# Equal units of 288 tokens in the first stage of an attention and two-layer MoE kernel, and phi with its token chunks innermost

## The chip, the cores and the metric

The kernel runs on one core of a Trainium2 chip. The metric is the device time of one execution in microseconds (us), the median of the runs shown. TensorE is called PE, its weight loads PEld, VectorE DVE, ScalarE ACT, GpSimd POOL; SP is the engine that issues all DMAs, and its queue is SPq.

## What is computed

```python
# q, k, v (8, 8, 576, 64); phi (8, 8, 576, 32)
a = exp(phi - max over s); a = a / sum over m
k_m = einsum('bhsm,bhsd->bhmd', a, k);  v_m likewise with v
attn = softmax(q @ k_m.T / 8) ; x = attn @ v_m      # 4608 tokens x 512
r = max(x @ w_in, 0); x = (s * r * r + b) @ w_out   # 512 -> 2048 -> 512
h = x @ w1; x = (h * sigmoid(1.702 h)) @ w2         # 512 -> 2048 -> 512
```

## The kernel before

Four stages follow one another on the core, each overlapping a little with the next. **Stage 1** goes over the 8 batches of 576 tokens. For each batch `slots` (L420) takes the softmax weights of phi and the 32 slots of every head, `attend` and `weigh` (L487, L514) make the attention weights of all 576 tokens as two tiles `ah` and `al` (the value split into a high and a low half in fp32r), `matrix` (L561) multiplies v_m by a fourth of w_in into `mh` and `ml`, and `step` (L581) multiplies the two and applies relu. A step is one pair of 128-column groups of the 2048 hidden columns (8 pairs, `pi`) and one unit of tokens: 12 matmuls by `mm3` (L276), which takes three products (high by high, high by low, low by high) for two groups and two halves of the contraction. The result `h` in PSUM is copied with relu to an SBUF tile `r` (L598) and written to DRAM. **Stage 2** (`down` with w_out, L622) reads r back in 12 blocks of 384 tokens, two at a time, squares them on ACT (L642) and multiplies by w_out with seven products instead of eight on 2x2 blocks; the operands A, B, C, D and E are such blocks of r. **Stage 3** (`up`, L731) and **stage 4** (`down` with w2) work on the same blocks of 384.

The order of work is made by `Order` (L31): every piece has a due time and a cost in each engine that may do it, and a list scheduler places them, holding back what finds no free buffer. It writes one fixed order for each engine, and each engine keeps to it. In this planner a matmul costs n / 2.4 + 13.4 ns for n columns (L246). Tiles come from pools by tag: 31 of tag "t" (r, the operands, kv, q and others), 30 of "w", 4 of "ps" in PSUM (L180).

The blocks of 384 tokens of stage 2 do not meet the 576 tokens of a batch, so `units` (L216) cuts each batch where a block ends: even batches into 384 and 192 tokens, odd ones into 192 and 384. A unit of 384 is a whole block in DRAM, one of 192 half of one:

```python
n = min(self.TS - t % self.TS, self.S * (b + 1) - t)
to = ("r", s, pi % 4, pi // 4, half)
self.dram(*to).rearrange("p (a t) -> p a t", a=2)[:, :, at:at + n]
```

`load` (L618) brings a whole block of 384 KB back with one DMA. In `slots` phi comes as [128 tokens, 4 heads, 5 chunks of tokens, 32 slots]; `fmx` (L429) takes the maximum over the 5 chunks through a view that steps 32 numbers, `sub` (L433) subtracts the maximum, and `mm` (L449) takes the 32 slots of a chunk and head, contiguous, as the stationary operand for 40 matmuls with k and v. Batch 0's scores are made in two groups, the first unit first; all later batches make both units at once.

Of the kernel before, what the change touches and what calls it, by code (L numbers as in the profile page):

```python
# [152 lines left out]
class Net:  # L153
# [35 lines left out]
    def __init__(self, nc, tc, ctx, aps):  # L189
        self.nc, self.tc, self.a = nc, tc, aps  # L190
        self.B, self.S = aps["q"].shape[0], aps["q"].shape[3]
        self.sb = ctx.enter_context(tc.tile_pool(name="sb", bufs=1))
        self.ps = ctx.enter_context(tc.tile_pool(name="ps", bufs=1, space=PSUM))
        self.dr = ctx.enter_context(tc.tile_pool(name="dr", bufs=1, space=bass.MemoryType.DRAM))
        self.n = self.spare = 0
        self.T = {}
        self.order = Order(self.BUFS)
        self.d = {}
# [16 lines left out]

    def units(self, b):  # L216

        t = self.S * b
        while t < self.S * (b + 1):
            n = min(self.TS - t % self.TS, self.S * (b + 1) - t)  # L220
            m = t // self.TS
            yield t - self.S * b, n, m // 2, m % 2, t % self.TS
            t += n
# [196 lines left out]
    def slots(self, b, g, due, lead=8):  # L420
# [5 lines left out]
        pm, pb, z, tr = (("ps", ("s", b, g, i)) for i in range(4))  # L426
        self.dma(d - lead, lambda: self.t(ph, [P, 4, 5, 32]), lambda: self.a["phi"][b, g], (), (ph,), 320)

        def fmx():  # L429
            nc.vector.tensor_reduce(self.t(mx, [P, P]).rearrange("p (h m) -> p h m", h=4),  # L430
                                    T[ph].rearrange("p h c m -> p h m c"), axis=AX.X, op=ALU.max)

        def sub():  # L433
            pbv = T[pb][:, 0, 0:P].rearrange("p (h m) -> p h m", h=4).unsqueeze(2).to_broadcast([P, 4, 5, 32])
# [14 lines left out]
        def mm():  # L449
            out = self.pst(z)  # L450
            n = self.S - 4 * P
            for c in range(5):
                for h in range(4):
                    s = slice(32 * h, 32 * h + 32)
                    if c < 4:
                        nc.tensor.matmul(out[s, 0, 0:129], T[ph][:, h, c, :], T[fs[h]][:, c], start=(c == 0), stop=False)
                    else:
                        nc.tensor.matmul(out[s, 0, 0:129], T[ph][0:n, h, c, :], T[f1][0:n, h], start=False, stop=True)

# [120 lines left out]

    def step(self, b, pi, u, unit, due):  # L581
        nc, T = self.nc, self.T
        h, r = ("ps", ("h", b, pi, u)), ("t", ("r", b, pi, u))
        j = pi // 2
        c0, n, s, half, at = unit
        c = slice(c0, c0 + n)
        m = [("w", (x, b, j)) for x in ("mh", "ml")]
        ats = [[("t", (x, b, k)) for x in ("ah", "al")] for k in range(2)]

        def mm():  # L590
            out = self.pst(h)
            for i in range(2):
                o = slice((2 * pi + i) % 4 * P, (2 * pi + i) % 4 * P + P)
                self.mm3(out[:, i, 0:n], [([T[x][:, k, o] for x in m], [T[x][:, c] for x in ats[k]]) for k in range(2)])

        self.pe(due, n, mm, (*m, *((*x, u) for k in ats for x in k)), (h,), count=12)
        self.order.add(due + 0.5, [
            self.act(2 * n, lambda: nc.scalar.activation(self.two(r, n=n), T[h][:, :, 0:n], AF.Relu), psum=True),  # L598
            self.dve(2 * n, lambda: nc.vector.tensor_scalar(self.two(r, n=n), T[h][:, :, 0:n], 0.0, None, op0=ALU.max))], (h,), (r,))
# [17 lines left out]

    def load(self, due, k, name, *index):  # L618
        r = [x for x in self.order.wrote if x[:1 + len(index)] == (name, *index)]
        self.dma(due, lambda: self.two(k).rearrange("p a b -> p (a b)"), lambda: self.dram(name, *index), r, (k,), 384)  # L620

# [109 lines left out]
    def up(self, s, due):  # L731
# [4 lines left out]
        for j, k in ((0, 0), (1, 0), (0, 1), (1, 1)):  # L736
            self.load(due - 26 + 2 * j + 4 * k, R[j, k], "x", s, j, k)
        r11, r12, r21, r22 = R[0, 0], R[0, 1], R[1, 0], R[1, 1]
# [86 lines left out]
    def plan(self):  # L825
# [8 lines left out]
        for b in range(B):  # L834
# [5 lines left out]
            for j in range(4):  # L840
# [119 lines left out]
```

## Time and profile before

| | us |
|---|---|
| median of 3 runs | 1403.19 |
| lowest, highest | 1402.94, 1405.13 |
| the profiled execution | 1407.16 |
| its span in the trace | 1405.2 |
| PE busy | 1381.0 (98%) |
| DVE busy | 1041.4 (74%) |
| ACT busy | 795.8 (57%) |
| DMA queue of SP, share of 16 engines | 71.0% |

PE is busy nearly all of the span, but its time is the sum of matmuls of several shapes, and a busy PE need not be at its peak: the ends of matmuls are modelled and neighbours overlap, so that what one costs is the distance from its start to the start of the next. Stage 1 lasts until about 350 us on PE, with matmuls of stage 2 mixed in from about 330 us.

### The profile page before, as it was taken

The numbers are of one execution on the slowest core, as the hardware profiler recorded it, in microseconds if no ns is written. First come the engines' busy times: TensorE is split into PE (matmuls) and PEld (weight loads), VectorE is DVE, ScalarE is ACT, GpSimd is POOL, SyncE is SP. The second block draws the span as 40 slices with busy tenths as digits, with TensorE's granted clock in tenths as the row PEclk, the third lists the DMA queues.
The fourth block names the chain that finished last, engine by engine and source line by source line (L and its number), as shares of the span: only waits on it lengthen the run. The fifth ranks groups of instructions, "written<-read, shape, count | busy, mean of one in ns | idle before, by whom it ended". The sixth has DMA issues, their size and how long they took to land.

```text
span 1405.2 us, 23985 instructions
## 1 busy us (share of the span) xinstructions
PE 1381.0 (98%) x9250; PEld 1328.2 (95%) x9250; DVE 1041.4 (74%) x1411; ACT 795.8 (57%) x1113; POOL 92.0 (7%) x70
## 2 busy tenths in 40 slices
PE   7899999999999999999999999999999999999998
PEld 6788888789999999999999999999999999999998
DVE  6959898786698888988876756565356967869682
ACT  4456665576677787687745655554335434434341
POOL 1401110100100100000110110100000000000000
PEclk9999999999999999999999999999999999999999
DMA  9979999899875585499979674764896465344541
GB/s 349 305 255 302 378 368 332 291 311 358 280 246 187 182 277 173 153 320 320 337 261 345 259 271 166 257 238 147 277 360 242 155 195 177 125 158 162 195 138 45
DMA packets 134576, 347.74 MB, mean 247 GB/s; under 512 B 14400, under 2 KB 30784, under 8 KB 134464
## 3 DMA queue, kind: packets, MB, share of 16 engines
q1 hardware_dynamic: 134464, 346.24, 71.0%
q8 instruction: 72, 1.18, 0.3%
q14 instruction: 40, 0.33, 0.1%
HBM read 211.44 MB, written 134.74 MB: 246 GB/s over the span
## 4 chain that ended last, share of the span: by engine, by line
PE 85%; DMA 7%; DVE 6%; ACT 1%; issue 1%; SPq 1%; ACTq 0%; DVEq 0%
PE X L667 9%; PE X L669 9%; PE X L668 9%; PE Y L668 4%; PE Y L669 4%; PE Y L667 4%; PE X L774 4%; PE X L775 4%; PE X L776 4%; PE h L280 4%; PE h L282 4%; PE h L281 4%; PE Z L669 2%; PE Z L667 2%; PE Z L668 2%; DMA w<-w 2%
## 5 line engine op out<-in xcount | busy, mean ns | idle before, releaser
L282 PE MATMUL h<-ah,ml 128*128 128x384 f32 (+1 forms) x512 | 157.1, 307 | 5.5 <-DVE ml L264 5.5
L280 PE MATMUL h<-ah,mh 128*128 128x384 f32 (+1 forms) x512 | 161.0, 314 | 0.8 <-ACT km L258 0.5
L264 DVE TENSOR_TENSOR u<-Y,u 128x768 f32<-128x768 f32 x60 | 57.4, 956 | 135.5 <-ACT u L782 69.5
L281 PE MATMUL h<-al,mh 128*128 128x384 f32 (+1 forms) x512 | 156.6, 306 | 0.7 <-DVE al L264 0.7
L667 PE MATMUL X<-oh,wo 128*128 128x384 f32 x384 | 129.2, 337 | 2.9 <-ACT u L693 2.9
L774 PE MATMUL X<-oh,w 128*128 128x384 f32 x384 | 128.5, 335 | 1.1 <-ACT a L782 0.7
L668 PE MATMUL X<-ol,wo 128*128 128x384 f32 x384 | 129.0, 336 | 0.0
L669 PE MATMUL X<-oh,wo 128*128 128x384 f32 x384 | 128.8, 336 | 0.0
L776 PE MATMUL X<-oh,w 128*128 128x384 f32 x384 | 128.3, 334 | 0.0
L775 PE MATMUL X<-ol,w 128*128 128x384 f32 x384 | 128.3, 334 | 0.0
L667 PE MATMUL X<-oh,w 128*128 128x384 f32 x384 | 128.3, 334 | 0.0
L668 PE MATMUL X<-ol,w 128*128 128x384 f32 x384 | 128.3, 334 | 0.0
L669 PE MATMUL X<-oh,w 128*128 128x384 f32 x384 | 128.3, 334 | 0.0
L598 ACT ACTIVATE r<-h 128x768 f32<-128x768 f32 (+1 forms) x127 | 82.4, 651 | 67.6 <-PE h L282 54.9
L258 ACT CAST oh<-C 128x768 fp32r<-128x768 f32 x93 | 76.4, 835 | 67.2 <-PE X L669 26.0
L280 PEld LDWEIGHTS h<-ah,mh 128*128 128x128 f32 x512 | 97.8, 191 | 17.5 <-issue 6.3
L264 DVE TENSOR_TENSOR ol<-A,oh 128x768 fp32r<-128x768 f32 x96 | 91.9, 967 | 17.0 <-PE X L668 7.1
L282 PEld LDWEIGHTS h<-ah,ml 128*128 128x128 f32 x512 | 97.4, 190 | 6.6 <-DVE ml L264 6.6
L281 PEld LDWEIGHTS h<-al,mh 128*128 128x128 f32 x512 | 97.4, 190 | 1.6 <-DVE al L264 1.6
L264 DVE TENSOR_TENSOR ol<-C,oh 128x768 fp32r<-128x768 f32 x96 | 90.8, 956 | 8.1 <-ACT oh L258 4.0
L264 DVE TENSOR_TENSOR ol<-E,oh 128x768 fp32r<-128x768 f32 x48 | 45.8, 957 | 61.6 <-PE Y L668 21.4
L322 POOL TENSOR_TENSOR cw<-cw,raw 128x512 uint32<-128x512 uint32 x32 | 47.0, 1469 | 579.6 <-DVE cw L319 365.3
(192 smaller groups left out, 3725.7 us busy)
## 6 DMA issues: line engine op xcount, KB each, us to landing
w<-w SPq DMA_DIRECT2D x112, 512.0 KB, 5.6
r<-r SPq DMA_DIRECT2D x64, 384.0 KB, 5.2
wo<-wo SPq DMA_DIRECT2D x42, 512.0 KB, 6.0
g<-u SPq DMA_DIRECT2D x48, 384.0 KB, 3.2
kv<-in_kv SPq DMA_DIRECT2D x64, 258.0 KB, 5.3
raw<-in_w SPq DMA_DIRECT2D x32, 512.0 KB, 5.2
r<-r SPq DMA_DIRECT2D x64, 192.0 KB, 5.0
q<-in_q SPq DMA_DIRECT2D x32, 288.0 KB, 5.5
```

Source lines behind the costliest of these rows:

```text
L258: self.order.add(due, [self.act(n, lambda: nc.scalar.copy(out(), src()), psum), self.dve(n, lambda: nc.vector.tensor_copy(out(), src()), f ...
L264: self.order.add(due, [self.dve(n, lambda: nc.vector.tensor_tensor(out(), a(), b(), op=op), port=port)], r, w, first)
L280: self.nc.tensor.matmul(ps, wh, xh, start=start and i == 0, stop=False)
L281: self.nc.tensor.matmul(ps, wh, xl, start=False, stop=False)
L282: self.nc.tensor.matmul(ps, wl, xh, start=False, stop=(i == n - 1))
L598: self.act(2 * n, lambda: nc.scalar.activation(self.two(r, n=n), T[h][:, :, 0:n], AF.Relu), psum=True),
L667: nc.tensor.matmul(out, T[w][:, 0, c], T[h][:, p], start=f, stop=False, skip_group_check=True)
L668: nc.tensor.matmul(out, T[w][:, 0, c], T[l][:, p], start=False, stop=False, skip_group_check=True)
L669: nc.tensor.matmul(out, T[w][:, 1, c], T[h][:, p], start=False, stop=last, skip_group_check=True)
L774: nc.tensor.matmul(out, T[w][:, 0, c], T[h][:, k], start=f, stop=False, skip_group_check=True)
L775: nc.tensor.matmul(out, T[w][:, 0, c], T[l][:, k], start=False, stop=False, skip_group_check=True)
L776: nc.tensor.matmul(out, T[w][:, 1, c], T[h][:, k], start=False, stop=k == 1, skip_group_check=True)
```

## The change

Every batch is cut into two equal units of 288 tokens. `step` writes each as a DRAM tile of its own, 128 rows of 576 numbers, contiguous. Stage 2 still works on blocks of 384: `pieces` finds the two half blocks that a block is made of (288 and 96, 192 and 192, or 96 and 288 tokens), and `load` gathers them with two DMAs. phi lies in DRAM and SBUF with the 5 chunks innermost, so that `fmx` reads contiguously, and the matmuls take their stationary operand with a step of 5 numbers. The planner's cost for `fmx` falls from 1000 to 640 elements.

```diff
-    def units(self, b):
...
+    def pieces(self, m):
+        t, end = self.TS * m, self.TS * (m + 1)
+        while t < end:
+            u, at = divmod(t, self.HS)
+            n = min(self.HS - at, end - t)
+            yield u // 2, u % 2, at, t - self.TS * m, n
             t += n
...
-        self.dma(d - lead, lambda: self.t(ph, [P, 4, 5, 32]), ...
+        self.dma(d - lead, lambda: self.t(ph, [P, 4, 32, 5]), ...
...
-                                    T[ph].rearrange("p h c m -> p h m c"), axis=AX.X, op=ALU.max)
+                                    T[ph], axis=AX.X, op=ALU.max)
...
-        self.on_dve(d, 1000, fmx, (ph,), (mx,))
+        self.on_dve(d, 640, fmx, (ph,), (mx,))
...
-                        nc.tensor.matmul(out[s, 0, 0:129], T[ph][:, h, c, :], T[fs[h]][:, c], start=(c == 0), stop=False)
+                        nc.tensor.matmul(out[s, 0, 0:129], T[ph][:, h, :, c], T[fs[h]][:, c], start=(c == 0), stop=False)
...
-        at = [e[:2] for e in self.units(b)]
+        at = [(0, self.HS), (self.HS, self.HS)]
...
-        self.pe(due, n, mm, (*m, *((*x, u) for k in ats for x in k)), (h,), count=12)
+        self.pe(due, HS, mm, (*m, *((*x, u) for k in ats for x in k)), (h,), count=12)
...
-        to = ("r", s, pi % 4, pi // 4, half)
-        self.dma(due + 2, lambda: self.dram(*to).rearrange("p (a t) -> p a t", a=2)[:, :, at:at + n], lambda: T[r], (r,), ((*to, at),), n // 2)
+        to = ("r", b, pi % 4, pi // 4, u)
+        self.dma(due + 2, lambda: self.dram(*to, cols=2 * HS), lambda: T[r].rearrange("p a b -> p (a b)"), (r,), (to,))
...
+        ps = [(("r", b, i, j, u), t, c, n) for b, u, t, c, n in self.pieces(2 * s + half)]
+        def go():
+            x = self.two(k)
+            for at, t, c, n in ps:
+                nc.sync.dma_start(x[:, :, c:c + n], self.dram(*at).rearrange("p (a t) -> p a t", a=2)[:, :, t:t + n])
+        self.order.add(due, [("sync", 384 / 340, go, False)], [p[0] for p in ps], (k,))
...
-                    for u, unit in enumerate(self.units(b)):
-                        self.step(b, 2 * j + i, u, unit, d + B1 / 8 * (i + unit[0] / self.S))
+                    for u in range(2):
+                        self.step(b, 2 * j + i, u, d + B1 / 16 * (2 * i + u))
```

How the order on two engines changes. First PE, from the scores of batch 3 (`a`; batches count from 0) to the next `vw` of `matrix`; of the 16 or 12 matmuls that write one tile the first stands here, and the last field is the moving operand's size. Before:

```order
L508 MATMUL a_355_1886<-q_286_1525,km_323_1717 32x192
L508 MATMUL a_356_1895<-q_286_1525,km_323_1717 32x384
L280 MATMUL h_359_1913<-ah_278_1483,mh_333_1761 128x192
L280 MATMUL h_365_1940<-ah_278_1483,mh_333_1761 128x384
L280 MATMUL h_369_1963<-ah_278_1483,mh_333_1761 128x192
L280 MATMUL h_373_1986<-ah_278_1483,mh_357_1906 128x384
L574 MATMUL vw_381_2014<-wi_12_113,km_323_1717 32x512 x2
```

With the change:

```order
L509 MATMUL a_351_1881<-q_288_1537,km_321_1713 32x288
L509 MATMUL a_352_1890<-q_288_1537,km_321_1713 32x288
L281 MATMUL h_355_1907<-ah_274_1464,mh_329_1754 128x288
L281 MATMUL h_361_1935<-ah_274_1464,mh_329_1754 128x288
L281 MATMUL h_363_1954<-ah_274_1464,mh_329_1754 128x288
L281 MATMUL h_366_1977<-ah_274_1464,mh_353_1899 128x288
L575 MATMUL vw_371_1999<-wi_13_115,km_321_1713 32x512 x2
```

The sequence of pieces is the same; units of 192 and 384 columns in turn have become units of 288.

Then SP's queue at the start of stage 2 (E and A are blocks of r, wo a weight tile; the size is that of the part moved). Before:

```order
L253 DMA wo_904_4771<-wo_4_0_1764 128x1024
L253 DMA r_5_3_1_1_4789<-r_895_4737 128x768
L253 DMA E_907_4794<-r_0_0_1_1_928 128x768
L253 DMA A_909_4799<-r_1_0_0_0_1142 128x768
L253 DMA wo_911_4818<-wo_4_1_2417 128x1024
L253 DMA E_913_4836<-r_0_1_1_1_986 128x768
L253 DMA A_915_4841<-r_1_1_0_0_1207 128x768
L253 DMA wo_917_4858<-wo_4_2_2971 128x1024
```

With the change:

```order
L254 DMA wo_911_4869<-wo_4_1_2436 128x1024
L630 DMA E_913_4887<-r_0_0_1_1_922 128x2x192
L630 DMA E_913_4887<-r_1_0_1_0_1381 128x2x192
L254 DMA wo_915_4893<-wo_4_2_3037 128x1024
L630 DMA A_917_4910<-r_1_0_0_0_1117 128x2x96
L630 DMA A_917_4910<-r_1_0_0_1_1139 128x2x288
L630 DMA E_918_4927<-r_0_1_1_1_980 128x2x192
L630 DMA E_918_4927<-r_1_1_1_0_1466 128x2x192
L630 DMA A_920_4935<-r_1_1_0_0_1157 128x2x96
L630 DMA A_920_4935<-r_1_1_0_1_1200 128x2x288
```

Each load of a block has become two rows on the queue, one behind the other, and what stands behind them comes that much later in the queue: SP has 886 rows before and 1006 with the change.

## Rows read from the trace of the kernel before

**Rows 1.** The page, part 1: busy time, share and instructions of each engine.
```profile
PE 1381.0 (98%) x9250; PEld 1328.2 (95%) x9250; DVE 1041.4 (74%) x1411; ACT 795.8 (57%) x1113; POOL 92.0 (7%) x70
```

**Rows 2.** Windows: length, busy (x) PE, PEld, DVE, ACT, POOL; PEclk, DMA share, GB/s.
```profile
104.00:142.00 38.00, 37.34 (x374) 30.93 (x375) 35.98 (x62) 25.26 (x42) 6.02 (x4) 1.00 0.91 303
...
335.00:380.00 45.00, 42.10 (x260) 40.69 (x259) 28.22 (x39) 28.28 (x42) 7.02 (x4) 0.96 0.87 300
```

**Rows 3.** Waits of PE, whole run: total us, times, longest.
```profile
PE h L282 <- DVE ml L264: 5.5, 4, 4.0
PE X L667 <- ACT u L693: 2.9, 1, 2.9
...
PE h L281 <- DVE al L264: 0.7, 3, 0.4
```

**Rows 4.** Timeline of PE, 150 to 154: start us, length us, instruction.
```profile
149.98 0.28 PE L281 MATMUL h<-al,mh 128*128 128x192 f32 x1
...
151.10 0.27 PE L282 MATMUL h<-ah,ml 128*128 128x192 f32 x1
...
152.29 0.33 PE L280 MATMUL h<-ah,mh 128*128 128x384 f32 x1
...
153.16 0.34 PE L282 MATMUL h<-ah,ml 128*128 128x384 f32 x1
```

**Rows 5.** Timeline of PE, 302.6 to 306: matmuls of two columns, then the next.
```profile
302.85 1.86 PE L396 MATMUL sums<-ones,cs 128*128 128x2 f32 x16
304.58 0.42 PE L280 MATMUL h<-ah,mh 128*128 128x384 f32 x1
```

**Rows 6.** Groups by line and form, whole run: xcount | busy us, mean ns | idle before.
```profile
L280 PE MATMUL h<-ah,mh 128*128 128x384 f32 x256 | 88.5, 346 | 0.4 <-ACT mh L258 0.4
...
L280 PE MATMUL h<-ah,mh 128*128 128x192 f32 x256 | 72.5, 283 | 0.5 <-ACT km L258 0.5
...
L598 ACT ACTIVATE r<-h 128x768 f32<-128x768 f32 x64 | 51.9, 810 | 39.2 <-PE h L282 32.6 <-issue 2.3 <-DMA r<-r 1.8
...
L598 ACT ACTIVATE r<-h 128x384 f32<-128x384 f32 x63 | 30.8, 489 | 28.3 <-PE h L282 22.3 <-DMA r<-r 3.2 <-issue 1.1
...
L430 DVE TENSOR_REDUCE an<-ph 128x128 f32<-128x640 f32 x16 | 21.0, 1318 | 6.8 <-DMA ph<-in_phi 6.8
...
L456 PEld LDWEIGHTS s<-kv,ph 128*32 128x32 f32 x512 | 13.2, 109 | 3.8 <-issue 2.7 <-ACT ph L442 0.6
...
L551 DVE TENSOR_REDUCE a<-st 128x18 f32<-128x576 f32 x14 | 10.0, 717 | 0.0
```

**Rows 7.** Timeline of PE, from batch 2's scores to batch 2's first unit.
```profile
109.55 0.36 PE L280 MATMUL h<-ah,mh 128*128 128x192 f32 x1
...
124.27 0.44 PE L281 MATMUL h<-al,mh 128*128 128x384 f32 x1 [0.18 <-DVE al L264]
```

**Rows 8.** Timeline of PE at the start of stage 2.
```profile
371.90 0.69 PE L667 MATMUL X<-oh,wo 128*128 128x384 f32 x1 [2.90 <-ACT u L693]
```

**Rows 9.** The chain of waits at the start of stage 2: start us, us, what.
```profile
359.02 3.62 DMA E<-r
...
363.27 5.77 DMA A<-r
...
370.71 1.14 ACT u L693 x2
```

**Rows 10.** DMA, 320 to 340: packets, MB and rate.
```profile
DMA packets 3486, 8.14 MB, mean 407 GB/s; under 512 B 326, under 2 KB 1420, under 8 KB 3484
```

**Rows 11.** DMA, 600 to 640: packets, MB and rate.
```profile
DMA packets 4309, 13.16 MB, mean 329 GB/s; under 512 B 480, under 2 KB 480, under 8 KB 4305
```

**Rows 12.** Timeline of SP's queue, start of stage 2: loads of r being issued.
```profile
359.02 0.32 SPq L253 DMA_DIRECT2D E<-r  x1
...
367.92 0.32 SPq L253 DMA_DIRECT2D A<-r  x1
```

**Rows 13.** Waits of SP's queue, whole run.
```profile
SPq L253 <- PE X L669: 172.3, 62, 12.1
```

More of the change, by code (lines that the diff above doesn't have):

```diff
@@ L426, in slots @@
         pm, pb, z, tr = (("ps", ("s", b, g, i)) for i in range(4))
-        self.dma(d - lead, lambda: self.t(ph, [P, 4, 5, 32]), lambda: self.a["phi"][b, g], (), (ph,), 320)
+        self.dma(d - lead, lambda: self.t(ph, [P, 4, 32, 5]), lambda: self.a["phi"][b, g], (), (ph,), 320)
         def fmx():
             nc.vector.tensor_reduce(self.t(mx, [P, P]).rearrange("p (h m) -> p h m", h=4),
-                                    T[ph].rearrange("p h c m -> p h m c"), axis=AX.X, op=ALU.max)
+                                    T[ph], axis=AX.X, op=ALU.max)
         def sub():
-            pbv = T[pb][:, 0, 0:P].rearrange("p (h m) -> p h m", h=4).unsqueeze(2).to_broadcast([P, 4, 5, 32])
+            pbv = T[pb][:, 0, 0:P].rearrange("p (h m) -> p h m", h=4).unsqueeze(3).to_broadcast([P, 4, 32, 5])
             nc.vector.tensor_tensor(T[ph], T[ph], pbv, op=ALU.add)
-        self.on_dve(d, 1000, fmx, (ph,), (mx,))
+        self.on_dve(d, 640, fmx, (ph,), (mx,))
         self.pe(d + 1, 512, lambda: nc.tensor.transpose(self.pst(pm)[:, 0, 0:P], T[mx], self.ident), (mx,), (pm,))
@@ L455, in mm @@
                     if c < 4:
-                        nc.tensor.matmul(out[s, 0, 0:129], T[ph][:, h, c, :], T[fs[h]][:, c], start=(c == 0), stop=False)
+                        nc.tensor.matmul(out[s, 0, 0:129], T[ph][:, h, :, c], T[fs[h]][:, c], start=(c == 0), stop=False)
                     else:
-                        nc.tensor.matmul(out[s, 0, 0:129], T[ph][0:n, h, c, :], T[f1][0:n, h], start=False, stop=True)
+                        nc.tensor.matmul(out[s, 0, 0:129], T[ph][0:n, h, :, c], T[f1][0:n, h], start=False, stop=True)
         self.pe(d + 4, 3000, mm, (ph, *fs, f1), (z,))
@@ L578, in matrix, with step @@
         self.tt(due + 1, 1024, lambda: self.t(ml, [P, 2, 512], F32R), lambda: T[pm], lambda: T[mh].bitcast(F32), ALU.subtract, (pm, mh), (ml,))
-    def step(self, b, pi, u, unit, due):
-        nc, T = self.nc, self.T
+    def step(self, b, pi, u, due):
+        nc, T, HS = self.nc, self.T, self.HS
         h, r = ("ps", ("h", b, pi, u)), ("t", ("r", b, pi, u))
         j = pi // 2
-        c0, n, s, half, at = unit
-        c = slice(c0, c0 + n)
+        c = slice(u * HS, u * HS + HS)
         m = [("w", (x, b, j)) for x in ("mh", "ml")]
@@ L593, in mm @@
                 o = slice((2 * pi + i) % 4 * P, (2 * pi + i) % 4 * P + P)
-                self.mm3(out[:, i, 0:n], [([T[x][:, k, o] for x in m], [T[x][:, c] for x in ats[k]]) for k in range(2)])
-        self.pe(due, n, mm, (*m, *((*x, u) for k in ats for x in k)), (h,), count=12)
+                self.mm3(out[:, i, 0:HS], [([T[x][:, k, o] for x in m], [T[x][:, c] for x in ats[k]]) for k in range(2)])
+        self.pe(due, HS, mm, (*m, *((*x, u) for k in ats for x in k)), (h,), count=12)
         self.order.add(due + 0.5, [
-            self.act(2 * n, lambda: nc.scalar.activation(self.two(r, n=n), T[h][:, :, 0:n], AF.Relu), psum=True),
-            self.dve(2 * n, lambda: nc.vector.tensor_scalar(self.two(r, n=n), T[h][:, :, 0:n], 0.0, None, op0=ALU.max))], (h,), (r,))
-        to = ("r", s, pi % 4, pi // 4, half)
-        self.dma(due + 2, lambda: self.dram(*to).rearrange("p (a t) -> p a t", a=2)[:, :, at:at + n], lambda: T[r], (r,), ((*to, at),), n // 2)
+            self.act(2 * HS, lambda: nc.scalar.activation(self.two(r, n=HS), T[h][:, :, 0:HS], AF.Relu), psum=True),
+            self.dve(2 * HS, lambda: nc.vector.tensor_scalar(self.two(r, n=HS), T[h][:, :, 0:HS], 0.0, None, op0=ALU.max))], (h,), (r,))
+        to = ("r", b, pi % 4, pi // 4, u)
+        self.dma(due + 2, lambda: self.dram(*to, cols=2 * HS), lambda: T[r].rearrange("p a b -> p (a b)"), (r,), (to,))
     def operand(self, due, i, key, src, n):
@@ L616, in minus, with load @@
                 [k for k in (a, b) if k != out], (out,))
-    def load(self, due, k, name, *index):
-        r = [x for x in self.order.wrote if x[:1 + len(index)] == (name, *index)]
-        self.dma(due, lambda: self.two(k).rearrange("p a b -> p (a b)"), lambda: self.dram(name, *index), r, (k,), 384)
+    def load(self, due, k, name, s, i, j, half):
+        if name != "r":
+            at = (name, s, i, j, half) if name == "g" else (name, s, j, half)
+            self.dma(due, lambda: self.two(k).rearrange("p a b -> p (a b)"), lambda: self.dram(*at), (at,), (k,), 384)
+            return
+        nc, HS = self.nc, self.HS
+        ps = [(("r", b, i, j, u), t, c, n) for b, u, t, c, n in self.pieces(2 * s + half)]
[4 more added lines that the diff above has]
+        self.order.add(due, [("sync", 384 / 340, go, False)], [p[0] for p in ps], (k,))
     def down(self, name, src, s, due):
@@ L736, in up @@
         for j, k in ((0, 0), (1, 0), (0, 1), (1, 1)):
-            self.load(due - 26 + 2 * j + 4 * k, R[j, k], "x", s, j, k)
+            self.load(due - 26 + 2 * j + 4 * k, R[j, k], "x", s, None, j, k)
         r11, r12, r21, r22 = R[0, 0], R[0, 1], R[1, 0], R[1, 1]
@@ L936 @@
         "q": q.reshape(B, 2, half, S, D).transpose(0, 2, 1, 4, 3).reshape(B, half, P, S),
-        "phi": phi.reshape(B, 2, half, P, 5, M).transpose(0, 1, 3, 2, 4, 5),
+        "phi": phi.reshape(B, 2, half, P, 5, M).transpose(0, 1, 3, 2, 5, 4),
         "kv": tokens(kv[:, :, :4 * P], 4),
```

6 lines of the change are left out of this document (1 added, 5 removed).

## The prediction

> **What bounds the kernel now.** I read the page's busy times first: PE is busy 1381.0 us of the span of 1405.2 us [rows 1], so only what shortens PE's own work, or opens a wait on PE, moves the time. The windows show that this holds in stage 1 too: in a window of 38 us in its middle PE is busy 37.34 us at a granted clock of 1.00, which is the 2.4 GHz level, while DVE stands at 35.98 us and the DMA share at 0.91 [rows 2]. PE is the bound with two others close behind it. The waits of PE say where it gives time away: 5.5 us in four waits for `ml`, one of them of 4.0 us, in the first batch; 0.7 us in three waits for `al`; and 2.9 us in one wait for a copy on ACT, at the entry to stage 2 [rows 3].
>
> Then the timeline, for the distance from start to start, since a busy figure hides the pipelining. Ten matmuls of 192 columns take from 149.98 to 151.10: 0.112 us each. Five of 384 take from 152.29 to 153.16: 0.174 us each [rows 4]. At 2.4 GHz 384 columns are 160 ns, so the longer matmul pays 14 ns beside its columns, while 192 columns are 80 ns and the shorter one pays 32. Something else is as long as 112 ns, and the sums show it: sixteen matmuls of two columns, each with its own 128-column weights, take from 302.85 to 304.58, which is 0.108 us each [rows 5]. A matmul with new weights does not come faster than every 0.108 to 0.112 us, however few its columns. The units of 192 stand on that floor, and it is the one thing that this change can remove.
>
> **The change part by part.** The sum is made against the profiled execution, 1407.16 us, which lies 3.97 us above the median of 1403.19.
>
> *Equal units.* Matmuls of 384 and of 192 columns are as many: 256 each in the rows of L280 [rows 6], and as many for L281 and L282, so 768 pairs. A pair now takes 0.174 + 0.112 = 0.286 us. Taking 96 columns off the longer one at 2.4 GHz leaves 0.174 - 0.040 = 0.134 us, still above the floor, and two of them 0.268. The change saves 0.018 x 768 = **13.8 us** of PE time. Bounds: nothing, if 288 columns fall midway between the two (0.143); no more than 13.8 us, as a column can't take less than a cycle. I take 13.8, because a floor that two columns reach as well as 192 is a floor and not a slope.
>
> *What of it is lost in batch 0.* There PE waits for `ml` [rows 3], which waits for the conversion of w_in on DVE; faster matmuls wait longer. One eighth comes back: **+1.7 us**. The remaining seven batches keep 12.1 us, 1.73 each, if nothing else becomes late.
>
> *What is late next.* The chain on DVE from a batch's scores to its `al` runs beside the last units of the batch before it. From 109.55, just behind the scores, to the first matmul that needs `al`, at 124.27, PE has 14.7 us of cover and then waits 0.18 us [rows 7]. Three such changes of batch are on the edge [rows 3]. The cover shrinks by 14.7 / 38 x 1.73 = 0.67 us at each: **+2.0 us**. At the other changes of batch PE doesn't wait for `al` at all, and I charge nothing there.
>
> *The entry to stage 2.* There PE stood 2.9 us for a copy of X on ACT [rows 8], and the granted clock of that window falls to 0.96 [rows 2]. The chain goes back through ACT's squaring to the loads of E and A, which land 3.62 and 5.77 us after their issue [rows 9]. With the change PE comes some ten us sooner, the r tiles are freed sooner too, but each load is two DMAs. I charge **+2.0 us**, about two thirds of the stall again; the ends are -2.9, if the stall goes, and the whole of the gain so far, if the loads keep their time.
>
> *Prologue.* Of the DVE instructions between the first scores and the first `ml`, 15 treat the first unit and 8 the second. Now the first is 96 columns narrower and the second as much wider: 672 columns fewer, at the 717 ns for 576 of a reduction [rows 6] 0.8 us, which PE waits for: **-0.8 us**.
>
> *Edits at nothing.* The maximum over phi takes 1318 ns for 640 numbers with a step of 32, where a contiguous reduction takes 717 for 576 [rows 6]; at that rate it takes 797, and 16 of them give DVE 8.3 us back. None is charged to the path, since the phi chain is started more than half a batch ahead; if that were all on the edge, the +2.0 of the three changes of batch would go. The relus on ACT take 810 ns for 768 numbers and 489 for 384 [rows 6], so two of 650 take as long as the pair. The scores of a batch have the same columns in two equal parts. The writes of r move the same bytes in the same 128 DMAs, now in rows of 2304 bytes instead of 3072 and 768. Between 320 and 340, where 1094 packets lie between 512 bytes and 2 KB, the rate is 407 GB/s; between 600 and 640, with none of those, 329 [rows 10, 11]: rows of 768 bytes weren't what slowed it, and none is gained by longer ones. All this lies beside PE.
>
> *The loads of r.* 120 loads become 240 DMAs, in runs of 384 to 1152 bytes. By [rows 10] runs of 768 bytes cost nothing. Runs of 384 bytes stand in no row; were they at half speed, the 80 pieces of 96 columns, 96 KB each, would take 7.9 MB / 407 GB/s = 19 us more of the DMA engines over 350 us. The extra issues take SP 0.32 us each [rows 12], 38 us over stage 2. SP mostly stands waiting for PE to free a tile (172.3 us in 62 waits of one kind alone, [rows 13]), so I charge nothing and keep the rest for a rival.
>
> *The step of 5 in phi's weights.* A load of 32 columns takes 109 ns [rows 6] and goes on beside the matmuls before it. I charge nothing; the upper end is a rival.
>
> **Sum:** -13.8 + 1.7 + 2.0 + 2.0 - 0.8 = -8.9 us. The profiled execution would take 1398.3 us, and the median 1403.19 - 8.9 = **1394.3 us**.
>
> **The rivals.**
>
> *The loads set the entry to stage 2.* The gain arrives there and is waited away: E and A land when DMA lets them, and the DMA share is 0.87 in that window [rows 2]. For it: the chain is DMA, DMA, ACT [rows 9]. Against: 300 GB/s in that window against 407 in another [rows 2, 10]. Some 8 us come back: 1402 us; from 1399 on it counts as this case.
>
> *Spacing is a slope.* If 288 columns take 0.143 us, PE saves nothing, and only the prologue is left: 1402.4 us. The sums [rows 5] speak against it. The Trainium skill, "TensorE: Matmul & The Clock Gate", section "Back-to-back issue gap", gives 81 ns for 128 columns and 131 for 512 in a sustained stream, and a straight line between the two, my estimate, would make the pair cost the same cut either way; the trace's 174 ns for 384 lies far off that line. The same page's section "LDWEIGHTS" gives columns / 1.2, 107 ns for 128, which is the floor seen here.
>
> *Slower: SP's queue in stage 2.* At each of the six turns from one pair of blocks to the next four E and four A are issued, 8.9 us from first to last [rows 12]. Eight more issues of 0.32 us delay the last by 2.6 us. If PE waits that long each time, 15.4 us come on top: 1409.7 us. It decides from (8.9 + 2.8) / 6 = 1.95 us a turn. Against it: the queue waits more than it issues [rows 13].
>
> *Slower: strided weights.* 640 weight loads of phi come in 160 groups of four. If each took twice 109 ns and all of it showed, 17.4 us come on top: 1411.7 us. Against it: a load only shows where it outlasts the matmuls it lies beside. The Trainium skill, "SBUF — State Buffer", states that SBUF has lines of 16 bytes and that each access to a new one pays; by that page every one of these weights, 20 bytes apart, pays. The row of L430 against L551 agrees for DVE; no row shows it for a weight load.
>
> **How the numbers follow.** A measurement of this kernel can tell 0.2%, 2.8 us, from no change. The forecast's case has 0.72, from 1387 to 1399: the low end keeps 13.8 + 0.8 us, and a part of the stall on top. The entry to stage 2 has 0.13, half of it still faster by over 2.8 us; the slope 0.05, no change; SP's queue 0.07 and the weights 0.03, slower. Faster 0.72 + 0.07 + 0.01 = 0.80, same 0.06 + 0.04 + 0.01 = 0.11, slower 0.09. The range runs from 1387.0 to 1403.0: it takes in the first three cases and leaves out the two slower ones and the edges.
>
> **What would show it.** Right: matmuls of 288 columns 0.134 us apart; stage 1 shorter by about 10 us; waits for `al` up to 0.8 us at changes of batch; the wait of X for ACT at the entry to stage 2 between 3 and 6 us; L430 near 800 ns. Wrong: a distance of 0.143; a wait of 10 us or more at the entry; waits of X or Y in stage 2 six times over, each behind a square on ACT; groups of phi matmuls longer than before.

## The result, and the profile after

| | before | after |
|---|---|---|
| median, lowest to highest, us | 1403.35 (1402.94 to 1405.13, 4 runs) | 1389.83 (1388.13 to 1392.27, 4 runs) |
| ratio, 95% interval | | 0.9903 (0.9885 to 0.992) |
| the profiled execution, its span | 1407.16, 1405.2 | 1392.27, 1390.5 |

The change is faster by 13.5 us by the medians and by 14.9 us by the two profiled executions; the forecast was 8.9 us. The profiled execution of the kernel before lies 3.8 us above its median, that of the change 2.4 us. The page of the change, part 1:

```profile
PE 1365.2 (98%) x9244; PEld 1312.7 (94%) x9244; DVE 1032.8 (74%) x1406; ACT 796.6 (57%) x1118; POOL 89.1 (6%) x70
```

PE is busy 15.8 us less than before [rows 1] and is still the bound. The timeline of PE in stage 1 after the change (start us, length us, instruction) has the reason:

```profile
149.78 0.30 PE L281 MATMUL h<-ah,mh 128*128 128x288 f32 x1
...
152.96 0.29 PE L281 MATMUL h<-ah,mh 128*128 128x288 f32 x1
```

There are 24 steps between these two rows, 3.18 / 24 = 0.1325 us each, where [rows 4] had 0.174 and 0.112. The last matmul of stage 1 shows what that adds up to. Timeline of the kernel before:

```profile
352.02 0.33 PE L282 MATMUL h<-ah,ml 128*128 128x384 f32 x1
```

and after:

```profile
336.49 0.29 PE L283 MATMUL h<-ah,ml 128*128 128x288 f32 x1
```

Stage 1 ends 15.5 us sooner; in both kernels 48 matmuls of stage 2 stand ahead of this last one. PE's idle time up to it has hardly grown: 14.5 us before, 14.9 after. The waits of PE in the whole run after (total us, times, longest):

```profile
PE h L283 <- DVE ml L265: 5.8, 4, 3.6
...
PE X L680 <- DVE ol L265: 2.6, 4, 0.9
...
PE X L679 <- ACT u L705: 0.9, 1, 0.9
PE X L679 <- ACT oh L259: 0.8, 1, 0.8
...
PE h L282 <- DVE al L265: 0.4, 1, 0.4
```

Against [rows 3], the wait for `ml` is as it was and the three waits for `al` are one, but the single wait of X at the entry to stage 2 has made way for six waits of X inside stage 2, four of them between 484 and 521 us. The windows say the same. The entry after the change, 335 to 380 (columns as in [rows 2]):

```profile
335.00:380.00 45.00, 45.00 (x265) 45.00 (x264) 39.40 (x52) 32.60 (x48) 5.81 (x4) 1.00 0.95 314
```

PE has no gap there and the granted clock stays at 1.00, where before it had 42.10 us and 0.96. That 0.96 was one stretch behind the stall, at the lower of the two levels (1.2 GHz); the window 371.9 to 375.3 of the kernel before (length, PE busy, matmuls begun, PEclk, DMA share, GB/s):

```profile
371.90:375.30 3.40, 3.40 (x11) 0.50 1.03 392
```

Its 11 matmuls take 1.9 us at 0.174 us each, so that the half clock cost about 1.5 us. Then the 300 us from 390 to 690, which is stage 2 in both kernels (same columns). Before:

```profile
390.00:690.00 300.00, 299.75 (x1729) 1.00 0.72 244
```

After:

```profile
390.00:690.00 300.00, 295.47 (x1692) 1.00 0.75 238
```

PE is idle 4.53 us instead of 0.25, and begins 37 matmuls fewer: at 0.174 us, 6.4 us of progress lost. The last matmul of stage 2 gives the sum of entry and stage. Before:

```profile
702.82 0.33 PE L669 MATMUL Y<-oh,wo 128*128 128x384 f32 x1
```

After:

```profile
688.76 0.33 PE L681 MATMUL Y<-oh,wo 128*128 128x384 f32 x1
```

From the last matmul of stage 1 it is 350.80 us before and 352.27 after, 1.5 us longer, with the same matmuls between. So in the two profiled executions stage 1 gives 15.5 us, the entry a wait of 2.9 us [rows 3] and some 1.5 us of half clock, and stage 2 takes some 6 us back.

Where stage 2 loses it can be followed at one of its turns. The timeline of SP's queue after (x2: the two pieces of one load):

```profile
490.46 1.17 SPq L630 DMA_DIRECT2D D<-r  x2
...
498.52 1.28 SPq L630 DMA_DIRECT2D D<-r  x2
...
501.19 1.22 SPq L630 DMA_DIRECT2D D<-r  x2
```

ACT's timeline behind it:

```profile
508.11 0.85 ACT L654 ACTIVATE D<-D 128x768 f32<-128x768 f32 x1 [2.06 <-DMA D<-r]
...
511.34 1.56 ACT L259 CAST oh<-D 128x768 fp32r<-128x768 f32 x2
```

and PE's:

```profile
512.22 0.44 PE L679 MATMUL X<-oh,wo 128*128 128x384 f32 x1 [0.81 <-ACT oh L259]
513.22 0.44 PE L680 MATMUL X<-ol,wo 128*128 128x384 f32 x1 [0.56 <-DVE ol L265]
```

SP issues loads one behind the other at 1.2 us a pair; the last D is issued at 501.19, ACT's square waits 2.06 us for it, and PE waits for the cast behind that square. Before, one load of r took one issue, of 0.32 us in [rows 12] and 0.382 in the median of D.

### The profile page after: what moved, and what is told of

It reads as the page before. It is cut to its first block, busy times and chain, and to the rows that moved or that the text cites. A ratio compares the mean times of both kernels' runs of the same rounds, so it can differ in the third digit from the quotient of the medians.

```text
span 1390.5 us, 24257 instructions
## 1 busy us (share of the span) xinstructions
PE 1365.2 (98%) x9244; PEld 1312.7 (94%) x9244; DVE 1032.8 (74%) x1406; ACT 796.6 (57%) x1118; POOL 89.1 (6%) x70
## 4 chain that ended last, share of the span: by engine, by line
PE 85%; DVE 6%; DMA 5%; issue 1%; ACT 1%; SPq 1%; DVEq 0%; ACTq 0%
PE X L680 8%; PE X L679 8%; PE X L681 8%; PE X L786 5%; PE X L788 5%; PE X L787 5%; PE h L281 4%; PE Y L680 4%; PE Y L681 4%; PE Y L679 4%; PE h L283 4%; PE h L282 4%; PE Y L787 2%; PE Y L786 2%; PE Y L788 2%; PE Z L679 2%
## 5 line engine op out<-in xcount | busy, mean ns | idle before, releaser
L281 PE MATMUL h<-ah,mh 128*128 128x288 f32 x512 | 156.6, 306 | 1.0 <-ACT ah L259 0.4
L283 PE MATMUL h<-ah,ml 128*128 128x288 f32 x512 | 151.9, 297 | 5.8 <-DVE ml L265 5.8
L282 PE MATMUL h<-al,mh 128*128 128x288 f32 x512 | 151.4, 296 | 0.5 <-DVE al L265 0.4
L598 ACT ACTIVATE r<-h 128x576 f32<-128x576 f32 x128 | 83.1, 649 | 56.6 <-PE h L283 48.7
L265 DVE TENSOR_TENSOR ol<-A,oh 128x768 fp32r<-128x768 f32 x96 | 90.6, 955 | 15.8 <-PE X L680 8.3
```

Source lines behind the costliest of these rows:

```text
L265: self.order.add(due, [self.dve(n, lambda: nc.vector.tensor_tensor(out(), a(), b(), op=op), port=port)], r, w, first)
L281: self.nc.tensor.matmul(ps, wh, xh, start=start and i == 0, stop=False)
L282: self.nc.tensor.matmul(ps, wh, xl, start=False, stop=False)
L283: self.nc.tensor.matmul(ps, wl, xh, start=False, stop=(i == n - 1))
L598: self.act(2 * HS, lambda: nc.scalar.activation(self.two(r, n=HS), T[h][:, :, 0:HS], AF.Relu), psum=True),
```

## The experiments

Each ratio is against executions of the kernel before that were taken beside the run (their medians are 1403.04 to 1404.01), with a 95% interval. The columns on PE are for the window from 390 to 690; in e5 and e13 its last 8 to 9 us are stage 3 already. Stage 2 is the time from the last matmul of stage 1 to the last of stage 2, the entry included. The last column is the median time of SP on one issue of a load of D.

| run | us | ratio | PE idle, us | matmuls begun | stage 2, us | issue of D, us |
|---|---|---|---|---|---|---|
| before | 1403.35 | | 0.25 | 1729 | 350.80 | 0.382 |
| the change | 1389.83 | 0.9903 (0.9885 to 0.992) | 4.53 | 1692 | 352.27 | 0.602 (x2) |
| e1 units only | 1390.66 | 0.9914 (0.99 to 0.9927) | 2.18 | 1704 | 350.14 | 0.602 (x2) |
| e2 phi only | 1403.44 | 1.0 (0.999 to 1.001) | 0.22 | 1728 | 347.81 | 0.382 |
| e6 320 and 256 | 1398.5 | 0.9962 (0.9949 to 0.9974) | 7.78 | 1664 | 357.08 | 0.602 (x2) |
| e4 before, loads cut by token | 1411.44 | 1.0054 (1.0041 to 1.0068) | 3.55 | 1700 | 355.27 | 0.602 (x2) |
| e9 before, loads cut by row | 1404.68 | 1.0006 (0.9994 to 1.0019) | 0.61 | 1725 | 348.35 | 0.422 (x2) |
| e5 change, one DMA per load | 1385.6 | 0.9871 (0.9851 to 0.9891) | 0.24 | 1727 | 346.27 | |
| e3 change, cut at the write | 1392.09 | 0.9918 (0.9903 to 0.9932) | 0.23 | 1727 | 346.28 | 0.320 |
| e7 change, POOL issues half | 1395.91 | 0.9941 (0.9918 to 0.9964) | 3.46 | 1699 | 352.57 | 0.530 |
| e10 change, loads 4 us earlier | 1391.69 | 0.9911 (0.9897 to 0.9926) | 5.03 | 1685 | 349.28 | 0.602 (x2) |
| e12 before, one copy earlier | 1405.87 | 1.0015 (1.0006 to 1.0025) | 0.25 | 1729 | 347.99 | 0.382 |
| e11 change, r in chunks | 1391.47 | 0.9913 (0.9899 to 0.9927) | 0.59 | 1697 | 352.13 | 0.411 (x2) |
| e13 the same, operands in rows | 1386.25 | 0.9883 (0.9866 to 0.99) | 0.63 | 1723 | 346.89 | 0.422 (x2) |

In e10 24 matmuls of stage 3, some 4.2 us, moved behind the end of stage 2, so that its 349.28 is no gain. The kernels with the old order have the stall at the entry in their stage 2: 2.9 us before, 1.4 in e2, 2.5 in e4, 1.3 in e9, 1.6 in e12.

### The two halves of the change

**e1**, the change with phi in its old layout, in the same order on every engine:

```diff
-        self.dma(d - lead, lambda: self.t(ph, [P, 4, 32, 5]), ...
+        self.dma(d - lead, lambda: self.t(ph, [P, 4, 5, 32]), ...
...
-                                    T[ph], axis=AX.X, op=ALU.max)
+                                    T[ph].rearrange("p h c m -> p h m c"), axis=AX.X, op=ALU.max)
...
-                        nc.tensor.matmul(out[s, 0, 0:129], T[ph][:, h, :, c], ...
+                        nc.tensor.matmul(out[s, 0, 0:129], T[ph][:, h, c, :], ...
...
```

> The changed kernel with phi's old layout (chunks outside, read with a step of 32); the order on every engine is that of the changed kernel. Theory 1 (the whole gain is PE's floor under narrow matmuls, phi is beside the path): 1389 to 1391 us, the reduction at 1320 ns again, waits of PE for al still under 0.5 us. Rival (the 8 us that phi gave DVE are why the expected waits for al did not come): 1391.5 to 1394 us and up to 0.7 us of wait for al at three or more changes of batch.

**e2**, the kernel before with phi in its new layout: the same lines the other way round.

> The kernel before with phi's new layout alone; the order on every engine is that of the kernel before. Theory 1: 1402 to 1404 us, the stall at the entry to stage 2 still there, phi's weight loads near 138 ns against 109 and hidden. Rival (a freer DVE is what removed the stall at the entry and its half clock): 1398 to 1399 us, without the wait of X on ACT.

Measured: the units alone have the whole gain (1390.66), phi alone none (1403.44). The last matmul of stage 1 starts at 336.49 in e1 too. Stage 2, with the same loads as in the change, lost less in e1's profiled execution (25 matmuls instead of 37), so that part of this loss seems to vary from one execution to the next. phi's instructions did change; the groups by form with the change:

```profile
L457 PEld LDWEIGHTS s<-kv,ph 128*32 128x32 f32 x512 | 14.4, 138 | 3.3 <-issue 2.1 <-ACT ph L443 0.7
...
L431 DVE TENSOR_REDUCE an<-ph 128x128 f32<-128x640 f32 x16 | 13.0, 813 | 7.8 <-DMA ph<-in_phi 7.8
```

The maximum went from 1318 to 813 ns and the strided weight load from 109 to 138 ns [rows 6]. Neither reaches PE's path.

### The floor under a matmul

**e6**, the change with units of 320 and 256 tokens.

```diff
+        self.U = (320, 256)
...
-        at = [(0, self.HS), (self.HS, self.HS)]
+        at = [(0, self.U[0]), (self.U[0], self.U[1])]
...
```

> The changed kernel with units of 320 and 256 tokens instead of 288 and 288. If a matmul costs the greater of 0.112 us and its columns at 2.4 GHz and 13 to 14 ns, 320 and 256 columns take 0.147 and 0.120 us, together the 0.267 of twice 288: 1389 to 1392 us. If the floor bends earlier (weights not fully hidden under 256 columns), 256 columns take 0.126 or more and the time is 1394 us or more.

Timeline of PE in e6:

```profile
149.21 0.31 PE L285 MATMUL h<-al,mh 128*128 128x320 f32 x1
...
150.38 0.28 PE L284 MATMUL h<-ah,mh 128*128 128x256 f32 x1
...
151.70 0.28 PE L286 MATMUL h<-ah,ml 128*128 128x256 f32 x1
```

Eight steps from 149.21 to 150.38 are 0.146 us each, eleven from 150.38 to 151.70 0.120: a pair takes 0.266, like two of 288. Down to 256 columns one pays the columns and some 13 ns; the floor of 0.112 lies below. The distances came as expected and stage 1 ended at 337.62; the time didn't (1398.5 instead of 1389 to 1392), since stage 2 lost more than with the change (7.78 us idle). Why it lost more no run took apart.

### What in the gathered loads costs

**e4**, the kernel before with each load of r cut by token into two DMAs, and **e9**, the same cut by row of the tile (each run has one of the two loops):

```diff
...
+            x = self.two(k)
+            for c in (0, 192):    # e4
+                self.nc.sync.dma_start(x[:, :, c:c + 192], self.dram(name, *index).rearrange("p (a t) -> p a t", a=2)[:, :, c:c + 192])
+            for c in (0, 1):      # e9
+                self.nc.sync.dma_start(x[:, c], self.dram(name, *index)[:, 384 * c:384 * c + 384])
...
```

> The kernel before with each load of r in two DMAs of 192 KB (half of the tokens of both rows); the order on every engine is otherwise that of the kernel before. Theory 1: 1407 to 1409 us, with waits of PE of about 1 us spread over stage 2. Rival (the number of DMAs does not matter): 1402 to 1404 us.

> The kernel before with each load of r in two DMAs of 192 KB, cut by row instead of by token, so that each DMA has one contiguous run of 1536 bytes per partition; order otherwise that of the kernel before. Theory 1a (what costs is SP's time for an issue, 0.32 us for one run per partition and 0.58 for two): an issue takes 0.32, a pair about 0.7 instead of 1.2, and the time is 1404 to 1407 us, under half of what the cut by token lost. Rival 1b (what costs is the number of DMAs in flight): 1409 to 1412 us as with the cut by token.

Issues of D on SP's queue (min/median/max ns, first and last start) in e4:

```profile
L627 SPq DMA_DIRECT2D D<-r x48: 518/602/971, 310.0 to 642.6; - x48
```

and in e9:

```profile
L627 SPq DMA_DIRECT2D D<-r x48: 319/422/963, 309.7 to 633.6; - x48
```

The number of DMAs and their bytes are the same. What differs is that a piece cut by token has two runs in each partition, one for each of the two rows of the tile, and a piece cut by row has one. With two runs SP spends at least 0.518 us on an issue, with one 0.319. The cut by token costs 7.6 us by its ratio, and its 1411.44 lies above the 1407 to 1409 expected; the cut by row can't be told from no change. The waits of PE from 380 to 700 in e4 are of the kinds that the change has:

```profile
PE X L677 <- DVE ol L264: 1.8, 3, 0.7
PE X L676 <- ACT oh L258: 1.5, 1, 1.5
```

**e5**, the change's order with one DMA of 384 KB per load. It reads product tiles made from w_out in place of r, so that stage 2 works on other numbers.

```diff
-            for at, t, c, n in ps:
-                nc.sync.dma_start(x[:, :, c:c + n], self.dram(*at).rearrange("p (a t) -> p a t", a=2)[:, :, t:t + n])
...
+            nc.sync.dma_start(x.rearrange("p a b -> p (a b)"), self.dram(*o, cols=1024)[:, 0:768])
```

> The changed kernel with one DMA of 384 KB for each load of r, which brings the same bytes from DRAM tiles of w_out's products instead of the two pieces of r: stage 2 computes on other numbers. The order on PE, DVE, ACT and POOL is that of the changed kernel. Theory 1 (the gather costs stage 2 its 5 to 6 us): 1384 to 1386 us, 292 us for the same stretch of stage 2 as before instead of 298. Rival (the new order costs them): 1389 to 1391 us.

Measured: 1385.6. Its window from 390 to 690:

```profile
390.00:690.00 300.00, 299.76 (x1727) 1.00 0.69 239
```

PE is idle 0.24 us, as before the change. With the change's order and without the gather the loss of stage 2 is gone. The gather costs 1389.83 - 1385.6 = 4.2 us by the medians, whose intervals overlap a little (0.9851 to 0.9891, 0.9885 to 0.992), and 352.27 - 346.27 = 6.0 us by the lengths of stage 2.

### Moving the cost instead of removing it

**e3**, the change with the cut at the write: a unit of 288 goes in one or two pieces into whole blocks, 192 writes instead of 128, and each load is one DMA again.

```diff
-self.dma(due + 2, lambda: self.dram(*to, cols=2 * HS), lambda: T[r].rearrange("p a b -> p (a b)"), (r,), (to,))
+while t < end:
+    n = min(self.TS - t % self.TS, end - t)
...
+    self.dma(due + 2, lambda to=to, t=t, n=n: self.dram(*to).rearrange("p (a t) -> p a t", a=2)[:, :, t % self.TS:t % self.TS + n],
+             lambda o=o, n=n: T[r][:, :, o:o + n], (r,), ((*to, t % self.TS),), n)
...
```

> The changed kernel, but a unit of 288 is written in one or two pieces into whole blocks of 384 (192 writes instead of 128 in stage 1), and stage 2 loads a block with one DMA again. Theory 1 (the doubled DMAs of stage 2 cost the 5 to 6 us that the trace shows lost between 390 and 690): 1383 to 1386 us, PE in stage 2 without the waits of about 1 us. Rival (stage 2 lost them by its new order and start, not by the number of DMAs): 1388 to 1391 us. Second rival (64 more writes block SP in stage 1): over 1392 us.

Measured: 1392.09. Stage 2 has no stall left, but the writes now have two runs per partition. SP's issues of them in e3:

```profile
L254 SPq DMA_DIRECT2D r<-r x184: 512/542/1913, 59.6 to 348.0; - x184
```

and in the change, where every write is one run:

```profile
L254 SPq DMA_DIRECT2D r<-r x122: 319/326/1502, 59.8 to 337.5; - x122
```

The last matmul of stage 1 starts at 344.18 instead of 336.49, and what stage 2 gains is lost there. Of these 7.7 us, 3.5 are lost at one place, where PE waits for kv (242.07) and, behind it, for nm (243.78); the granted clock from 220 to 260 is 0.96 there, in the change 1.00. That the writes are what made this load late is likely and not shown: in stage 1 SP waits 40.2 us for the relu of r where the change has 102.2, so its queue is fuller. 0.75 us of the 7.7 are older than the first write.

**e7**, the second piece of each load issued by POOL; **e10**, the change's loads of r due 4 us earlier.

```diff
-            for at, t, c, n in ps:
-                nc.sync.dma_start(x[:, :, c:c + n], self.dram(*at).rearrange("p (a t) -> p a t", a=2)[:, :, t:t + n])
+            for e, (at, t, c, n) in zip((nc.sync, nc.gpsimd), ps):     # e7
+                e.dma_start(x[:, :, c:c + n], self.dram(*at).rearrange("p (a t) -> p a t", a=2)[:, :, t:t + n])
...
-                self.load(d - 14 - 2 * (x == 1), t, src, s, q, j, k)
+                self.load(d - 14 - 2 * (x == 1) - 4 * (src == "r"), t, src, s, q, j, k)   # e10
```

> The changed kernel with the second piece of each load issued from POOL's queue instead of SP's. Theory 1a (SP's issue time costs): SP is relieved of 120 issues of 0.58 us; 1384 to 1387 us if POOL issues in time. Rival: POOL's own issues are slow or hold back its additions for w1, and PE waits in stage 2 as before or longer: 1389 to 1400 us.

> The change's kernel with each load of r due 4 us earlier. If the gathered loads cost stage 2 only by standing later on SP's queue, an earlier due time gives back part of it: stage 2 at 293 to 296 us instead of 298.2 and 1386 to 1388.5 us. Rival (SP's time is what is short, so whatever goes ahead delays other transfers, and buffers come free no earlier): 298 us or more, and 1389 to 1393 us.

Both missed the gain. The six times of e7 run from 1391.89 to 1399.61 us, and its trace is of the shortest. POOL's issues in it are longer (0.72 us), and they come late, as its timeline at the same turn shows:

```profile
501.07 0.72 POOL L630 DMA_DIRECT2D B<-r  x1 [1.71 <-DMA B<-r]
502.25 0.73 POOL L630 DMA_DIRECT2D D<-r  x1 [0.46 <-issue]
```

The last D is issued no sooner than with SP alone (501.19), since POOL's queue has waits of its own between its pieces; so this run halves SP's work on the loads without showing what that is worth. In e10 the idle time stays (5.03 us): the rival held, an earlier place in the order does not shorten the queue.

### The entry to stage 2

**e12**, the kernel before with ScalarE's copy of X moved ahead of the second square of E and the square behind it:

```diff
...
+            fns.remove(f)                              # the copy u of the first block
+            fns.insert(fns.index(self.behind), f)      # ahead of the square of the second E
...
```

> The kernel before with one copy (u, out of the sums X) moved on ScalarE ahead of the second E square and the A square behind it; nothing else moves on any engine. Theory (the entry stall of the kernel before is ScalarE's order: the copy stands behind a square that waits for a late load, and PE's next X matmul waits for the copy; the clock then falls): the wait of X for ScalarE at 371.9 us and the half clock after it are gone, 3 to 5 us less, 1398.5 to 1400.5 us. Rival (the load itself is what is late, and the next operand waits for it wherever the copy stands): the stall only moves to the matmuls behind it, 1402 to 1403.5 us.

The copy now stands ahead of the last twelve matmuls that add to X, so it leaves their products out, and those twelve wait for it. Timeline of ACT in e12:

```profile
361.45 0.85 ACT L644 ACTIVATE E<-E 128x768 f32<-128x768 f32 x1 [2.30 <-DMA E<-r]
...
363.51 1.21 ACT L699 ACTIVATE u<-X,bw,sc 128x384 f32<-128x384 f32 x2
```

and of PE:

```profile
364.78 0.44 PE L673 MATMUL X<-oh,wo 128*128 128x384 f32 x1 [1.64 <-ACT u L699]
```

The stall moved from one square that waits for its load to another and kept 1.64 us. The clock didn't fall, but that is no effect of the move: e2 and e9 have the old order, waits of 1.4 and 1.3 us there, and a granted clock of 1.00 too. The time is no better than before (1405.87, above both expectations). The run doesn't settle whether ACT's order or the lateness of the loads makes the stall.

### A layout without the second run

**e11**, the change with r kept in chunks of 96 tokens, the two rows of a chunk side by side. Half a block, a quarter and three quarters are then each one run per partition; the relu writes this layout and the matmuls of stage 2 read their 384 columns as four pieces.

```diff
+    def chunks(self, x):
+        return x.rearrange("p a b -> p (a b)").rearrange("p (c a t) -> p a c t", a=2, t=96)
...
-                nc.sync.dma_start(x[:, :, c:c + n], self.dram(*at).rearrange("p (a t) -> p a t", a=2)[:, :, t:t + n])
+                nc.sync.dma_start(x.rearrange("p a b -> p (a b)")[:, 2 * c:2 * (c + n)], self.dram(*at)[:, 2 * t:2 * (t + n)])
...
```

> The change's kernel with r laid out in chunks of 96 tokens, two rows of a chunk side by side (the relu writes it so, and the matmuls of stage 2 read it so), so that each piece of a gathered half block is one run per partition instead of two. Order on every engine as in the change, same number of DMAs. Theory (an issue costs SP by its runs per partition, about 0.32 us for one run and 0.58 us for two, and that is what delays stage 2): an r load issues at 0.32 to 0.42 us, a pair at about 0.7 us instead of 1.21, stage 2 lasts 292 to 294 us instead of 298.2, and the time is 1385 to 1387.5 us. Rival (two DMAs per load or the shorter runs themselves are the cost): stage 2 stays at 296 us or more and the time at 1389 to 1392. Second rival (matmuls whose moving columns lie in four pieces of 96 are slower than 0.174 us): 1400 or more.

The stalls went (0.59 us idle) but not the time. The timeline of PE in e11 shows why:

```profile
560.13 0.34 PE L685 MATMUL X<-oh,wo 128*128 128x384 f32 x1
...
561.90 0.34 PE L686 MATMUL X<-ol,wo 128*128 128x384 f32 x1
```

Ten steps are 1.77 us, 0.177 each instead of 0.174: columns in four pieces cost some 0.003 us a matmul, and 2016 of them 6 us. The second rival had the mechanism and overrated its price.

**e13**, the same, with the casts and subtractions writing the operands in rows again.

```diff
+            plain = lambda x: x.rearrange("p a (c t) -> p a c t", t=96)
+            self.hi(due, n, lambda: plain(self.two(h, F32R)), lambda: self.chunks(T[src]), (src,), (h,))
...
```

> As the run with r in chunks of 96, but the casts and the subtractions that make the operands of stage 2 write them in rows again, so that the matmuls read 384 columns that lie together. Order on every engine as in the change. That run showed no stall left in stage 2 (0.6 us of waits on PE) but spaced its 2016 matmuls at 0.175 to 0.178 us instead of 0.173 to 0.174. Theory (the stalls were SP's issue time, and the 0.003 us a matmul are the price of the columns in four pieces): both are gone, stage 2 lasts 291.5 to 293.5 us, and the time is 1384 to 1387 us. Rival (the casts and subtractions that permute take so much longer that DVE and ScalarE come late in stage 2 instead): stage 2 at 296 us or more and 1389 us or more. Second rival (the operands are not what the spacing depends on): spacing still 0.176 us, stage 2 at 297 us.

Measured: 1386.25 us, 0.9883 (0.9866 to 0.99), the fastest of the versions that compute all of it. The window and the issues of D in e13:

```profile
390.00:690.00 300.00, 299.37 (x1723) 1.00 0.71 239
```

```profile
L638 SPq DMA_DIRECT2D D<-r x48: 319/422/1092, 300.2 to 617.1; - x48
```

The square that stood at 508.11 in the change, 2.06 us behind its load, is here:

```profile
503.77 0.85 ACT L662 ACTIVATE D<-D 128x768 f32<-128x768 f32 x1 [1.19 <-DMA D<-r]
```

It still waits, but PE no longer does there. The casts that permute take 829 to 833 ns in the mean of each operand, as they do in the change. Against the change the medians are 3.6 us apart, 2.8 by the ratios; the two intervals overlap (0.9866 to 0.99, 0.9885 to 0.992), so that this gain is likely and not proven by the times alone. That the stalls went is shown by the trace.

## Why the prediction was right, and where it wasn't

The time, 1389.83, lies in the range and 4.5 us below the forecast, and the mechanism, equal units above the floor, was the right one: e1 has it all. The terms:

- **Equal units, -13.8: held, and gave a little more.** Predicted 0.134 us a matmul, measured 0.1325. A pair then saves 0.286 - 0.265 = 0.021 us, and 768 pairs 16.1 us, above the 13.8 that I took for the most it could be; PE is busy 15.8 us less, and stage 1 ends 15.5 us sooner. e6 shows from the other side that the spacing is columns plus a constant, down to the floor. The rival that spacing is a slope (0.143) falls.
- **Lost again in batch 0, +1.7: no such loss.** The waits for `ml` are 5.8 us against 5.5 [rows 3], 0.3 us more. Why they didn't grow with the faster matmuls no run took apart; the prologue's -0.8 us lies in the same waits and can't be told from it.
- **The chain of `al`, +2.0: the step failed.** I shortened the cover and left the chain as it was. The chain from a batch's scores to its `al` got shorter too. On PE and then on DVE at the start of batch 2, before:

```profile
108.44 1.18 PE L508 MATMUL a<-q,km 64*32 64x384 f32 x32
```

```profile
122.27 0.38 DVE L316 TENSOR_SCALAR cwo<-cwo 128x512 uint32<-128x512 uint32 x1
...
122.87 0.68 DVE L319 SCALAR_TENSOR_TENSOR cwo<-raw,cwo 128x512 uint32<-128x512 uint32 x1
123.47 0.75 DVE L264 TENSOR_TENSOR al<-aT,ah 128x576 fp32r<-128x576 f32 x1
```

and after:

```profile
105.10 1.20 PE L509 MATMUL a<-q,km 64*32 64x288 f32 x32
```

```profile
114.99 0.42 DVE L314 TENSOR_SCALAR cwo<-cwo 128x512 f32<-128x512 f32 x1
115.32 0.75 DVE L535 TENSOR_REDUCE a<-st 128x18 f32<-128x576 f32 x1
...
119.22 0.74 DVE L265 TENSOR_TENSOR al<-aT,ah 128x576 fp32r<-128x576 f32 x1
```

From 15.03 to 14.12 us, 0.9 us less where the forecast took 0.67 off the cover: what was late before is a little less late. The rows show where the 0.9 went. Among the chain's own instructions DVE also has other work. Two pieces that make `ml` stand there in both kernels; beside them there are, before, three pieces from 122.27 to 123.47, 1.2 us, and after, one from 114.99 to 115.32, 0.33 us. The order on DVE had moved with the units, and it was fixed before the kernel ran. phi's cheaper maximum isn't the cause, since e1 ends stage 1 at the same time without it. How late the chain comes differs between executions: e5 and e13, with the same order, wait 1.4 us in two waits for `al` where the change waits 0.4 us in one.

- **The entry to stage 2, +2.0: wrong sign.** The stall is gone, my lower end of -2.9, and with it the half clock. ACT's timeline at the entry before:

```profile
368.16 0.85 ACT L642 ACTIVATE E<-E 128x768 f32<-128x768 f32 x1 [3.29 <-DMA E<-r]
...
370.62 1.23 ACT L693 ACTIVATE u<-X,bw,sc 128x384 f32<-128x384 f32 x2
```

and after:

```profile
349.71 0.85 ACT L654 ACTIVATE E<-E 128x768 f32<-128x768 f32 x1 [2.45 <-DMA E<-r]
351.38 1.23 ACT L705 ACTIVATE u<-X,bw,sc 128x384 f32<-128x384 f32 x2 [0.82 <-PE X L681]
```

A load of E is late in both. Before, the copy `u` stands behind four squares, the late E one of them; after, it stands behind one square, and it is the copy that waits for PE. That it is this order, and not the earlier arrival, was not shown: e12 failed to separate the two. A part of the 2.9 us, and the half clock with it, belonged to the profiled execution alone: in e2 and e9, with the old order there, the wait is 1.4 and 1.3 us and the granted clock stays at 1.00.
- **The loads of r, 0: wrong, some 4 to 6 us.** I took an issue at 0.32 us, the row of a load in one run, and held that SP mostly waits. A piece with two runs takes 0.518 at least and 0.602 in the median, a pair 1.2 us. What seems to count is not the mean load of the queue but its stretch at a turn, where the loads stand in a row; that it is SP's time, and not the shorter runs, is likely and not settled (see the end). The rival of SP's queue had the place, behind squares on ACT, and likely the mechanism, and overrated the price: 15.4 us, where the windows show 6.4 and e5 4.2. The number that I lacked stood in the trace before, in the writes of r, half of them half a block and so two runs per partition (issues on SP's queue, min/median/max ns):

```profile
L253 SPq DMA_DIRECT2D r<-r x123: 319/524/1632, 58.8 to 355.7; - x123
```

- **phi, 0: held.** 138 ns for a strided weight load against 109, 813 ns for the maximum against the 797 forecast, and no effect on the time (e2). The Trainium skill, "SBUF — State Buffer", section "Specifications (TRN2)", states that SBUF has lines of 16 bytes and that an access to a new one pays. The weight load agrees, 1.27 times as long; it lies beside other matmuls, and the time doesn't feel it.

So the sum came near by luck, through errors that cancel: -8.9, less 5.7 us of losses that didn't come, less 2.3 us that the units gave beyond 13.8, less a stall of 1.4 to 2.9 us, plus 4.2 to 6.4 us that weren't counted, gives -11.9 to -15.6 us, with -13.5 measured. The signs say the same. Of those for being right, the distance of the matmuls came and the maximum near 800 ns, stage 1 gained more than 10 us, and the waits at the changes of batch and at the entry didn't come; of those for being wrong, the six waits of X in stage 2 came, though not one at each turn.

## What to carry to other kernels

Matmuls that each bring new weights have a floor (here 0.108 to 0.112 us); cut the moving side into equal pieces above it, and read the floor off the shortest matmuls that the trace has. Then cost a DMA's issue by the contiguous runs it has in each partition (here 0.32 us for one and 0.52 for two), not by its bytes: choose the layout in memory so that every cut that a reader makes falls between whole runs. And when a stage gets faster, read in the new order what stands in the chains that race it before charging them for the lost cover.

## What the runs showed of the hardware that was not expected

- One issue on SP's queue took 0.319 us at least with one run in each of 128 partitions, 0.512 to 0.518 with two (e3, e4, e9). On POOL a piece with two runs took 0.720 us at least (e7).
- That the cost comes from SP's time on the issue, and not from what the DMA engines make of shorter runs, is likely and not settled: the two go together in every run here. In the window from 390 to 690 e4 moves its data in 62445 DMA packets and e9 in 37943, the change in 58836 and e13 in 36454.
- A matmul of 384 columns that lie in four pieces of 96, 768 bytes apart, took 0.177 us instead of 0.174 (e11). ACT's casts with such an operand took no longer: 829 to 833 ns in e13 and in the change.
